# Five o tiles transposed by TensorE, seven loads moved on the SP queue, one projection moved ahead of the steps, in the first attention of a four-layer kernel

## The chip, the cores and the metric

The kernel runs on one core of a Trainium2 chip. The metric is the device time of one launch in microseconds. The time before is 1161.44 us, the median of three runs (1160.57, 1161.44, 1164.82). One further execution was profiled; all rows quoted below come from it.

Names of the engines: PE is TensorE (PEld are its weight loads), DVE is VectorE, ACT is ScalarE, POOL is GpSimd, SP is SyncE. SP, ACT and POOL also issue DMAs; "SPq" marks work on SP's queue.

## What is computed

Two kinds of layer in the order A, B, A, B, each with a layernorm in front and a residual around it, on x of 2048 rows and 576 columns in bf16. A is an attention of 32 heads of 18 columns in which each position sees itself and seven earlier positions at a distance of two. B is a gated MLP with a spatial projection.

```python
def _A_ref(x, wqkv, wo):
    B, S, D = x.shape
    H = 32
    Dh = D // H
    W, dil = (8, 2)
    qkv = (lambda x, *d: x.transpose(*d))((x @ wqkv).reshape(B, S, 3, H, Dh), 2, 0, 3, 1, 4)
    q, k, v = (qkv[0], qkv[1], qkv[2])
    ...
    logits = jnp.einsum('bhsd,bhswd->bhsw', q, kg) * scale
    logits = jnp.where(mask[None, None, :, :], logits, -1000000000.0)
    attn = _softmax(logits, axis=-1)
    o = jnp.einsum('bhsw,bhswd->bhsd', attn, vg)
    return (lambda x, *d: x.transpose(*d))(o, 0, 2, 1, 3).reshape(B, S, D) @ wo

x = A_x
x = x + _A_ref(_layernorm(x, axis=-1), A_wqkv, A_wo)
x = x + _B_ref(_layernorm(x, axis=-1), B_w_in, B_w_sp, B_b_sp, B_w_out)
x = x + _A_ref(_layernorm(x, axis=-1), A_wqkv, A_wo)
x = x + _B_ref(_layernorm(x, axis=-1), B_w_in, B_w_sp, B_b_sp, B_w_out)
```

## The kernel before

The attention layer (`layer_A`, called with `li` 0 and 2) sets the order of every engine by hand: within it each engine executes its instructions in the order in which the Python code emits them, and waits where an operand isn't there. The first call, `li == 0`, is the one that the change touches. It has three parts.

*The prologue.* x comes in by rows (`x_load`), is normalised on DVE (`S_`, `R_`, `A_`) and turned into `xnT`, tiles 0 to 3 by TensorE (`T_pe`), tiles 4 to 15 by DMA transposes on SP (`T_`, L306). `PG` (L482) projects q and k: one unit is a block `d` of 128 of the 576 columns, `qk` (0 or 1, q or k), and a chunk `cc` of 512 positions; it is five matmuls on TensorE (L462) and a copy into a staging buffer (L443 on DVE, L445 on ACT). Blocks 0 to 2 are staged in `stg`, block 3 of the second half in a buffer called `x_in` in the rows, block 4 and the first half's block 3 in a part of `win2a` that is lent out until its weights are loaded. When the last unit of a block is staged, its heads are moved by eight or so DMAs into `QK`, where each head has 18 of 32 partitions; these are issued alternately by POOL and SP (rows `QK<-stg`, `QK<-x_in`, `QK<-win2a`). The other 14 partitions hold a pattern that masks the window; DVE writes it in two halves (`fill_window_rows`, L201), after a load of the pattern (`win_pat`). `VW` projects v (L451).

A DMA's issue on POOL or SP waits until the DMA issued eight places before it by that queue kind has landed: there are eight completion semaphores on each.

*The steps.* The sequence is cut into 17 query tiles, one of 128 and sixteen of 120 positions; a step `s` (0 to 33) is half the heads of tile `s // 2`. Each step emits the logits of the next step (`L_mm`, 16 matmuls, L536) and their `EXP` on ACT (L545), then its own `PV` (16 matmuls, L559), after which DVE takes the reciprocal of the sums (L565) and writes o into one of four buffers `o_t` (L567); and then what a table holds for that step. The logits lie in PSUM in tag X (three banks, one buffer) and Y (one bank, two buffers). All else that TensorE writes (`O_ps`, `pp`, `pv`, `pw`, `pt`) takes turns on three banks, PT, during the steps. In the table stand:

- `PG`, the projections of the second half of the positions, one per step in steps 0 to 11, after six such units (`pre`) ahead of step 0; the order is (4,0,2), (3,1,2), (3,0,2) and then blocks 0, 1, 2, 3, 4 of the last chunk. The logits need the second half from step 16 on: step 16 takes blocks 0 to 2, step 17 blocks 2 to 4.
- `VW`, the rest of v, from step 12 on.
- `WO`, the output projection (L627, rows `pw`), from step 13 on, two halves per row tile, and behind it on DVE the residual sum (L630) and layernorm statistics (L638), on POOL the normalisation (L299), on SP the stores (`XST`, `XN_ST`); near the end SP reads the normalised rows back through DMA transposes (`LN_T`, L669) as `xnT` of the next layer, whose first matmuls are the rows `hh` (L234).
- `O_CP`: see next.

o has to be transposed for `WO`, into a ring `oT` of 768 columns. After the second half step of tile `t`, SP issues a DMA transpose of `o_t`: where the tile's first position is a multiple of 16 (tiles 0, 1, 3, 5, ...) right into the ring (L574, all 128 columns, of which the last eight belong to the next tile), otherwise into one of two slots (L578), from which DVE copies it some steps later (`O_CP`, L587). Only the last two tiles are transposed by TensorE (`O_T`, L593: five 128-column pieces into one PSUM bank, then a copy on ACT, L595).

*Loads.* At step 0 the table issues on SP the first three `XO` loads (rows of x for the residual, into `xo` and a part of `x_in`), and then `load_wo`. Two of the six pieces of `win2a`, weights of layer B that lie outside the part lent out, are loaded in the prologue from POOL's queue, between `R_(6, 2)` and the normalisation of tiles 6 and 7.

*After the steps* the tail of `WO` runs, and TensorE goes on with layer B.

Of the kernel before, what the change touches and what calls it, by code (L numbers as in the profile page):

```python
# [63 lines left out]
class K:  # L64
# [316 lines left out]
    def layer_A(self, li):  # L381
        nc, tc, cfg = self.nc, self.tc, self.cfg
        S, NT, XW, NS = cfg.S, cfg.NT, cfg.XW, cfg.NS
# [20 lines left out]
        oT = main.tile([P, 5, RING * P], bf16, name="oT")  # L404
# [17 lines left out]
        def tdim(t):  # L422
            return P, cfg.tiles[t][1]

        def q0_(t):
            return cfg.tiles[t][0]
# [14 lines left out]
        def evac(out, in_, dve):  # L441
            if dve:
                nc.vector.tensor_copy(out=out, in_=in_)  # L443
            else:
                nc.scalar.copy(out=out, in_=in_)  # L445
# [102 lines left out]
        def in_ring(t):  # L548
            return q0_(t) % 16 == 0

        def PV(s):
            t, hf = divmod(s, 2)
            nk, nq = tdim(t)
            O_ps = self.PT_tile([P, 512], f32, "O_ps")
            for jp, js in enumerate(((0, 1, 2), (3,))):
                for ftl in range(4):
                    for jj, j in enumerate(js):
                        idx = 4 * ftl + j
                        nc.tensor.matmul(O_ps[:, idx * (DH + 1):(idx + 1) * (DH + 1)],  # L559
                                         lhsT=P_bufs[2 * jp + s % 2][:nk, jj, ftl, :],  # L560
                                         rhs=v_ext[:nk, t, 16 * hf + idx, :], start=True, stop=True)
            Ov = O_ps[:, 0:16 * (DH + 1)].rearrange("p (h e) -> p h e", e=DH + 1)
            o_t = o_bufs[t % len(o_bufs)]
            rec = sb.tile([P, 16], f32, name="rec", tag="rec", bufs=2)
            nc.vector.reciprocal(out=rec[:], in_=Ov[:, :, DH])  # L565
            LN_AGGR()
            nc.vector.tensor_tensor(out=o_t[:, 288 * hf:288 * (hf + 1)].rearrange("p (h d) -> p h d", d=DH),  # L567
                                    in0=Ov[:, :, 0:DH], in1=rec[:, :, None].to_broadcast([P, 16, DH]), op=ALU.mult)
            LN_POW()
            if hf == 1 and t < NT - 2:  # L570
                if in_ring(t):
                    c0 = q0_(t) % (RING * P)
                    n0 = min(P, RING * P - c0)
                    nc.sync.dma_start_transpose(out=oT[:, :, c0:c0 + n0], in_=o_t[0:n0, :])  # L574
                    if n0 < P:
                        nc.sync.dma_start_transpose(out=oT[:, :, 0:P - n0], in_=o_t[n0:P, :])
                else:
                    nc.sync.dma_start_transpose(out=o_slots[(t // 2) % NSLOT][:], in_=o_t[:, :])  # L578

        def ring_parts(t):  # L580
            nq, c0 = tdim(t)[1], q0_(t) % (RING * P)
            n0 = min(nq, RING * P - c0)
            return [(c0, 0, n0)] + ([(0, n0, nq - n0)] if n0 < nq else [])

        def O_CP(t):
            for c0, a, n in ring_parts(t):
                nc.vector.tensor_copy(out=oT[:, :, c0:c0 + n], in_=o_slots[(t // 2) % NSLOT][:, :, a:a + n])  # L587

        def O_T(t):
            nq = tdim(t)[1]  # L590
            pt = self.PT_tile([P, 5, P], bf16, "pt")
            for c in range(5):
                nc.tensor.transpose(pt[:, c, :nq], o_bufs[t % len(o_bufs)][:nq, c * P:(c + 1) * P], self.ident[:nq, :nq])  # L593
            for c0, a, n in ring_parts(t):
                nc.scalar.copy(out=oT[:, :, c0:c0 + n], in_=pt[:, :, a:a + n])  # L595

        tails = {}
        late_rows = []
# [5 lines left out]
        def xo_of(p):  # L604
            if li == 0:
                return p % 3
            return p % 2 if p < 4 else (2, 0, 1)[(p - 4) % 3]

        def XO(i):
            if i % 2 == 0:  # L610
                xo = xo_bufs[xo_of(i // 2)]
                src = self.rows_of(x_prev, i, 2) if li == 0 else x_prev[i * P:(i + 2) * P, :]
                self.dma(xo, src.rearrange("(a p) d -> p a d", p=P), eng=nc.sync)
                for k_ in range(2):
                    tails[i + k_] = dict(xo=xo[:, k_, :])
# [25 lines left out]
        def LN_AGGR():  # L641
            for i, st in owed:
                mv = sb.tile([P, 2], f32, name="ln_mv", tag="ln_mv", bufs=5)
                nc.vector.bn_aggr(out=mv[:], in_=st[:])
                tails[i]["ln"] = mv

        def LN_POW():
            for i, _ in owed:
                mv = tails[i]["ln"]
                rstd = sb.tile([P, 1], f32, name="ln_rstd", tag="ln_rstd", bufs=5)  # L650
                nc.vector.tensor_scalar(out=rstd[:], in0=mv[:, 1:2], scalar1=EPS, scalar2=None, op0=ALU.add)
                nc.gpsimd.tensor_tensor(out=rstd[:], in0=rstd[:], in1=self.neg_half[:], op=ALU.pow)
                tails[i]["ln"] = mv, rstd, None
            owed.clear()
# [19 lines left out]
        if li == 0:  # L674
# [54 lines left out]
            def A_(*tiles):  # L729
                for i in tiles:  # L730
                    xns[i] = xn = self.xn_bufs[self.xn_rr % len(self.xn_bufs)]
                    self.xn_rr += 1
                    nc.vector.tensor_scalar(out=xn[:, 0:D], in0=xts[i], scalar1=mvs[:, i, 0:1],
                                            scalar2=rstds[:, i:i + 1], op0=ALU.subtract, op1=ALU.mult)
# [36 lines left out]
            S_(6, 7)  # L771
            R_(6, 2)
            rows[3](nc.gpsimd)
            for f in self.load_win2a(nc.gpsimd)[4:6]:
                f()
            A_(6, 7)
            T_(6, 7)
            S_(8)
# [49 lines left out]
        def at(s, f, *a):  # L828
            table.setdefault(s, []).append((f, a))
        pgs = [(d, qk, cc) for d, cc in ((0, 2), (1, 2), (2, 2), (0, 3), (1, 3), (2, 3), (3, 2), (3, 3), (4, 2), (4, 3))  # L830
               for qk in ((1, 0) if d < 4 else (0,))]
        PG_END = 14
        pre, pgs = pgs[:6], pgs[6:]
        if li == 0:
            pgs = [u for u in pgs if u[2] == 2] + [u for u in pgs if u[2] > 2]
            pgs.insert(0, pgs.pop(2))
        for k_, (d, qk, cc) in enumerate(pgs):
            at(k_ if li == 0 else (k_ * PG_END) // len(pgs), PG, d, qk, cc, True, *((q2,) if li == 0 else ()))
        vws = [(t, hh) for t in range(nvw, NT) for hh in range(2)]
# [7 lines left out]
        units += [NST] * 3 + [NST + 1] * 2 + [NST + 2] * 2  # L847
        wo_steps = list(zip(units[0::2], units[1::2]))
        assert len(wo_steps) == NS
        for t in range(NT - 2):  # L850
            s = wo_steps[q0_(t) // P][0] - 1
            r = (q0_(t) + tdim(t)[1] - 1) // P - RING
            if t < NT - 3 and not in_ring(t):
                at(min(2 * t + 6, s), O_CP, t)
                assert r < 0 or wo_steps[r][1] < min(2 * t + 6, s)
            else:
                assert r < 0 or wo_steps[r][1] < 2 * t + 1
        tail_rows = []
        for i in range(NS):
            s, s1 = wo_steps[i]  # L860
            if i % 2 == 0:
                last = [j for j in range(i) if xo_of(j // 2) == xo_of(i // 2)][-1:]
                at(max([s - 7 if li > 0 or last else 0] + [wo_steps[j][1] + 1 for j in last]), XO, i)
            at(s, WO, i, 0)
            at(s1, WO, i, 1)
            if s1 < NST - 1:
                at(s1, LN_STATS, i)
                at(s1 + 1, LN_XN, i)
            else:
                tail_rows.append(i)  # L870
            at(s1 + 1, XST, i)
            if i < NS - 2:
                at(s1 + 4, XN_ST, i)
            if NS // 2 <= i < NS - 1:
                for k_ in range(2):
                    at(max(s1 + 6, NST + 3 * (i - NS // 2) - 4, NST + 4 if i > NS // 2 + 1 else 0), LN_T, 2 * i - NS + k_)
# [7 lines left out]
            at(NST + 3, XN_ST, i)  # L884
        at(2 * (NT - 3) + 4, O_CP, NT - 3)
        if li == 0:
            at(0, self.load_wo, nc.sync)
            for k_ in range(4):
                at(PG_END - 1 + k_ if k_ else 1, self.load_win2a((nc.gpsimd, nc.sync)[k_ % 2])[k_])
        s_b, d_b = (PG_END + 3, 2) if li == 0 else (PG_END + 1, 1)  # L890
        at(s_b, alloc_win2b)
        for k_ in range(6):
            at(s_b + d_b * k_, win2b_piece, k_)
        at(NST - 2, O_T, NT - 2)
        at(NST, O_T, NT - 1)
        for k_, (d, qk, cc) in enumerate(pre):
            if k_ == (2 if li == 0 else 0):
# [9 lines left out]
        for s in range(NST):  # L907
            if s == NST - 1:
                self.ring = ["PT", "PT", "PT", "Y", "Y"]
            if s + 1 < NST:  # L910
                L_mm(s + 1)
                EXP(s + 1)
            PV(s)
            for f, a in table.pop(s, []):
                f(*a)
# [339 lines left out]
```

## Time and profile before

| | us |
|---|---|
| median of three runs | 1161.44 |
| the profiled execution, its time | 1159.11 |
| its span, first to last instruction | 1157.3 |
| TensorE busy | 1144.1 |
| first attention, to the first `hh` matmul of layer B | 127.0 |
| begin of step 0's `PV` | 49.6 |

The page gives, for one execution, the busy time of each engine, the chain of work that ended last, followed back from the last instruction, and groups of instructions by line. A timeline row is start, length, engine, line, operation, output and inputs, count, and in brackets the idle time of the engine in front of it with what ended it. A row of the chain in order of time is start, length and what the time went to; "issue" there is time in which an engine waited for nothing that the profile shows. A row of windows gives for a stretch the busy time of PE, PEld, DVE, ACT and POOL with the number of their instructions, then the granted TensorE clock (1.00 is full speed), the mean busy share of the DMA engines (it can exceed 1 where queues overlap), and GB/s. A row of waits is who waited for whom: us in total, times, longest. Line numbers are those of the kernel before.

### The profile page before, as it was taken

What the parts mean: (1) busy time and instruction counts of PE and PEld (TensorE: products, weight loads), DVE (VectorE), ACT (ScalarE), POOL (GpSimd) and SP (SyncE); (2) the same over time, 40 slices, a digit from 0 to 9 for tenths busy, and PEclk for the clock granted to TensorE, in tenths of its full rate; (3) what the DMA queues carried; (4) which work ended last, traced back from release to release, by engine and by line L of the source; (5) the groups of instructions that cost most, each with busy time, mean ns of one, the idle gap of its engine ahead of it and who ended that gap; (6) DMA issues with size and microseconds to landing.
All of it is one profiled execution on the core that took longest, in us unless ns stands there. A gap on an engine that the chain in (4) does not pass through costs nothing.

```text
span 1157.3 us, 29603 instructions
## 1 busy us (share of the span) xinstructions
PE 1144.1 (99%) x12894; PEld 613.0 (53%) x12894; DVE 535.3 (46%) x1184; ACT 371.3 (32%) x665; POOL 260.3 (22%) x389
## 2 busy tenths in 40 slices
PE   8989999999999999999999999999999999999998
PEld 5557644444444444457755774544444444444676
DVE  8768898222232222334475889853322223222311
ACT  5588656111110111102247886641111111011000
POOL 3669855000000000001254676530000000000000
PEclk9999999999999999999999999999999999999999
DMA  8798797000000000049455786940000000000322
GB/s 212 141 179 216 163 208 153 24 12 12 13 2 12 12 12 1 1 131 228 109 104 104 173 174 155 213 108 1 12 12 13 13 11 3 12 1 29 101 74 58
DMA packets 184637, 93.07 MB, mean 80 GB/s; under 512 B 136180, under 2 KB 177812, under 8 KB 184506
## 3 DMA queue, kind: packets, MB, share of 16 engines
q1 hardware_dynamic: 171866, 71.96, 29.6%
q0 software_dynamic: 6048, 13.31, 4.6%
q10 hardware_dynamic: 6592, 5.90, 1.7%
q8 instruction: 101, 1.65, 0.6%
q14 instruction: 30, 0.25, 0.1%
HBM read 35.46 MB, written 14.69 MB: 43 GB/s over the span
## 4 chain that ended last, share of the span: by engine, by line
PE 93%; DMA 3%; POOL 1%; DVE 1%; issue 1%; ACT 1%; SPq 0%; DVEq 0%; ACTq 0%; POOLq 0%
PE hh L234 79%; PE pp L462 4%; PE pw L627 3%; PE O_ps L559 2%; PE pv L451 2%; PE L_ps L536 2%; DMA QK<-stg 1%; POOL QK L78 1%; DMA QK<-x_in 1%; DMA x_in<-in_A_x_dram 1%; PE L_ps L462 1%; ACT P_sb L545 1%; DMA xnT<-ln_xn 0%; PE hh L1177 0%; DVE ln_st L713 0%
## 5 line engine op out<-in xcount | busy, mean ns | idle before, releaser
L234 PE MATMUL hh<-Wq,Z 64*128 64x512 bf16 x4608 | 505.8, 376 | 0.0
L234 PEld LDWEIGHTS <-Z 64*128 64x128 bf16 x6984 | 340.1, 94 | 309.8
L1081 DVE TENSOR_TENSOR g_tmp<-hh,ln_xn 128x512 f32<-128x512 f32 x144 | 92.8, 686 | 452.4 <-PE hh L234 452.4
L933 ACT COPY bank_turn<-ones 1x1 bf16<-1x1 bf16 x239 | 44.7, 187 | 538.3 <-PE hh L234 538.3
L78 POOL DMA_DIRECT2D wout<-in_B_w_out_dram x4 | 4.3, 1073 | 602.0 <-PE hh L234 602.0
L234 PE MATMUL hh<-wout,Z 64*128 64x288 bf16 x2232 | 137.0, 283 | 0.0
L545 ACT ACTIVATE P_sb<-L_ps 128x1440 bf16<-128x1440 f32 (+3 forms) x136 | 125.1, 972 | 23.5 <-PE L_ps L536 22.0
L234 PE MATMUL hh<-xnT,w 64*128 64x512 bf16 x1152 | 132.2, 376 | 0.0
L234 PE MATMUL hh<-win2a,xnT 64*128 64x512 bf16 (+1 forms) x960 | 118.7, 355 | 0.0
L234 PEld LDWEIGHTS <-xnT 64*128 64x128 bf16 x1440 | 69.9, 94 | 70.0 <-issue 0.5
L1006 DVE BATCH_NORM_STATS2 z_st<-zp 128x6 f32<-128x512 bf16 (+1 forms) x160 | 92.6, 622 | 11.1 <-ACT zp L1004 11.1
L1072 ACT ACTIVATE z1T<-hh 128x1024 bf16<-128x1024 f32 x72 | 73.7, 1023 | 62.2 <-PE hh L234 62.2
L1082 DVE TENSOR_TENSOR Z<-g_tmp,z1T 128x512 bf16<-128x512 f32 x144 | 92.3, 682 | 0.0
L234 PEld LDWEIGHTS <-w 64*128 64x128 bf16 x1152 | 56.1, 94 | 68.3
L1004 ACT ACTIVATE zp<-hh 128x1024 bf16<-128x1024 f32 (+1 forms) x96 | 76.0, 809 | 48.9 <-PE hh L234 48.7
L462 PE MATMUL pp<-xnT,wqk_sb 128*128 128x512 bf16 (+1 forms) x330 | 75.9, 379 | 1.7 <-DMA xnT<-ln_xn 1.7
L234 PE MATMUL hh<-win2b,xnT 64*128 64x512 bf16 (+1 forms) x480 | 72.8, 355 | 0.0
L1146 DVE TENSOR_TENSOR x_new<-hh,xo 128x288 bf16<-128x288 f32 x64 | 26.3, 452 | 92.7 <-PE hh L234 85.0
L299 POOL TENSOR_SCALAR ln_xn<-x_new,ln_mv,ln_rstd 128x576 bf16<-128x576 bf16 x28 | 64.1, 2288 | 2.6
L78 POOL DMA_DIRECT2D QK<-stg x76 | 48.0, 634 | 41.4 <-DVE stg L443 16.3
L462 PEld LDWEIGHTS <-wqk_sb 128*128 128x128 bf16 (+1 forms) x360 | 31.9, 97 | 38.5 <-issue 4.1
L1030 POOL TENSOR_SCALAR Z<-zp,z_mv,z_rstd 128x256 bf16<-128x256 bf16 x32 | 51.1, 1597 | 3.5
(122 smaller groups left out, 745.9 us busy)
## 6 DMA issues: line engine op xcount, KB each, us to landing
xres<-x_new SPq DMA_DIRECT2D x44, 144.0 KB
wout<-in_B_w_out_dram POOLq DMA_DIRECT2D x4, 1296.0 KB, 7.9
xo<-xres SPq DMA_DIRECT2D x32, 144.0 KB
xn_rows<-ln_xn SPq DMA_DIRECT2D x28, 160.0 KB
w<-in_B_w_in_dram SPq DMA_DIRECT2D x16, 256.0 KB
QK<-stg POOLq DMA_DIRECT2D x51, 72.0 KB, 4.6
QK<-stg SPq DMA_DIRECT2D x37, 72.0 KB
xo<-in_A_x_dram SPq DMA_DIRECT2D x6, 288.0 KB
```

Source lines behind the costliest of these rows:

```text
L78: return eng.dma_start(out=out, in_=in_)
L234: ins = self.nc.tensor.matmul(outs[a_], lhsT=lhs(a_, c, r0), rhs=rhs(a_, c, r0), start=start and k_ == 0, stop=stop and k_ == len(chunks) ...
L299: e.tensor_scalar(out=xn[:nrows, 0:D], in0=x_t[:nrows, :], scalar1=mv[:nrows, 0:1], scalar2=rstd[:nrows, 0:1], op0=ALU.subtract, op1=ALU.mult)
L462: nc.tensor.matmul(pp, lhsT=w, rhs=self.xnT[r0:r1, c, cc * 512:(cc + 1) * 512], start=start, stop=stop, tile_position=(r0, 0))
L545: nc.scalar.activation(out=P_bufs[2 * jp + s % 2][:nk, :, :, 0:nq], in_=Lv[:nk, :, :, 0:nq], func=ACT.Exp, scale=scale)
L933: self.turn_on = lambda tok: nc.scalar.copy(out=tok, in_=self.ones[0:1, 0:1])
L1004: nc.scalar.activation(out=zp[:, w0:w0 + n], in_=pz, func=ACT.Gelu_apprx_tanh)
L1006: nc.vector.bn_stats(out=st[:, x // 512, :], in_=zp[:, x:x + min(512, w0 + n - x)])
L1030: eng.tensor_scalar(out=Z[:, b0:b1, i, :], in0=zv[:, b0:b1, :], scalar1=mv[:, 0:1], scalar2=rstd[:, 0:1], op0=ALU.subtract, op1=ALU.mult)
L1072: lambda ht, z1T=z1T, q2=q2: nc.scalar.activation(out=z1T[:, q2 * 512:(q2 + 2) * 512], in_=ht[:].rearrange("p a b -> p (a b)"), func=ACT.G ...
L1081: nc.vector.tensor_tensor(out=tmp[:], in0=pg[:, a_, :], in1=bsp[:, qs], op=ALU.add)
L1082: nc.vector.tensor_tensor(out=uT(jj)[:, sub, qs], in0=tmp[:], in1=z1Ts[jj, sub][:, qs], op=ALU.mult)
```

## The change

All of it holds for the first attention alone (`li == 0`). Tiles 2 to 6 get no DMA transpose and no `O_CP`; instead `O_T` runs for tile t at the end of step 2t + 2, its copy on DVE (two copies for tile 6, which wraps around the ring's end). One unit, (3,1,2), moves from step 1 of the table to the end of `pre`, so that the units left stand in steps 0 to 10, each one step earlier; being the seventh there, its copy is made by ACT. The first three `XO`, `load_wo` and the two pieces of `win2a` are issued on SP where the table is built, that is behind the row transposes of tiles 12 to 15 and ahead of `pre`; the two pieces of `win2a` leave POOL's queue.

```diff
-            if hf == 1 and t < NT - 2:
+            if hf == 1 and t < NT - 2 and t not in pe_turn:
                 if in_ring(t):
...
+        pe_turn = tuple(range(2, 7)) if li == 0 else ()
+
         def O_T(t):
             nq = tdim(t)[1]
             pt = self.PT_tile([P, 5, P], bf16, "pt")
             for c in range(5):
                 nc.tensor.transpose(pt[:, c, :nq], o_bufs[t % len(o_bufs)][:nq, c * P:(c + 1) * P], self.ident[:nq, :nq])
             for c0, a, n in ring_parts(t):
-                nc.scalar.copy(out=oT[:, :, c0:c0 + n], in_=pt[:, :, a:a + n])
+                evac(oT[:, :, c0:c0 + n], pt[:, :, a:a + n], t in pe_turn)
...
             rows[3](nc.gpsimd)
-            for f in self.load_win2a(nc.gpsimd)[4:6]:
-                f()
             A_(6, 7)
...
         pre, pgs = pgs[:6], pgs[6:]
         if li == 0:
+            pre.append((3, 1, 2))
+            pgs.remove((3, 1, 2))
+        if li == 0:
             pgs = [u for u in pgs if u[2] == 2] + [u for u in pgs if u[2] > 2]
-            pgs.insert(0, pgs.pop(2))
+            pgs.insert(0, pgs.pop(1))
...
+        for t in pe_turn:
+            at(2 * t + 2, O_T, t)
         for t in range(NT - 2):
             s = wo_steps[q0_(t) // P][0] - 1
             r = (q0_(t) + tdim(t)[1] - 1) // P - RING
-            if t < NT - 3 and not in_ring(t):
+            if t in pe_turn:
+                assert s >= 2 * t + 2 and (r < 0 or wo_steps[r][1] < 2 * t + 2)
+            elif t < NT - 3 and not in_ring(t):
                 at(min(2 * t + 6, s), O_CP, t)
...
                 last = [j for j in range(i) if xo_of(j // 2) == xo_of(i // 2)][-1:]
-                at(max([s - 7 if li > 0 or last else 0] + [wo_steps[j][1] + 1 for j in last]), XO, i)
+                if li > 0 or last:
+                    at(max([s - 7] + [wo_steps[j][1] + 1 for j in last]), XO, i)
+                else:
+                    XO(i)
...
         if li == 0:
-            at(0, self.load_wo, nc.sync)
+            self.load_wo(nc.sync)
+            for f in self.load_win2a(nc.sync)[4:6]:
+                f()
```

## The prediction

> **What bounds the kernel now.** I read the page's busy times first, then the windows of the first attention (0 to 127 us), then the chain of work in order of time there, and last the timelines of TensorE, DVE, GpSimd and SP around each wait.
>
> ```profile
> span 1157.3 us, 29603 instructions
> ...
> PE 1144.1 (99%) x12894; PEld 613.0 (53%) x12894; DVE 535.3 (46%) x1184; ACT 371.3 (32%) x665; POOL 260.3 (22%) x389
> ```
>
> TensorE is busy for 1144.1 of 1157.3 us. So an edit in the first attention can only remove TensorE's waits there, or its slow stretches, or add TensorE work. Behind the first attention TensorE's program is the same before and after, so I let a gain made there reach the end whole.
>
> The chain in order of time (start, length, what) shows the largest wait:
>
> ```profile
> 68.85 7.71 DMA QK<-stg
> ...
> 77.41 7.70 DMA QK<-x_in
> ...
> 85.16 0.23 PE L_ps L536 x4
> ...
> 86.51 1.17 PE pw L627 x5
> 87.68 0.52 PE L_ps L536 x16
> 88.20 0.53 PE O_ps L559 x16
> 88.73 1.21 PE pv L451 x5
> ...
> 90.56 0.32 PE L_ps L536 x16
> 90.89 0.50 PE O_ps L559 x16
> 91.38 0.63 PE pv L451 x5
> 92.01 0.61 PE pw L627 x5
> ```
>
> The logits of step 17 need the heads of projection block d=3 (staged in x_in), whose moves into QK land at 85.11. TensorE's own timeline (start, length, what, idle before and its releaser):
>
> ```profile
> 47.95 0.46 PE L536 MATMUL L_ps<-QK 32*128 32x128 bf16 x13
> 48.84 0.84 PE L536 MATMUL L_ps<-QK 32*128 32x128 bf16 x3 [0.44 <-DMA QK<-win2a]
> ...
> 74.74 0.39 PE L536 MATMUL L_ps<-QK 32*128 32x120 bf16 x16 [0.40 <-ACT P_sb L545]
> ...
> 81.50 0.39 PE L536 MATMUL L_ps<-QK 32*128 32x120 bf16 x7
> ```
>
> Those logits begin at 81.50 and end at 85.16 + 0.23 = 85.39; an undisturbed step takes 0.32 for them: 3.57 us lost. The rows behind are slow: 1.17 against 0.61, 0.52 against 0.32, 0.53 against 0.50, 1.21 against 0.63, together 1.37 us; the granted clock of that window, 0.57, shows why. The hole costs 4.94 us. In these windows the busy times are followed by the granted clock, the DMA share and GB/s:
>
> ```profile
> 50.00:54.00 4.00, 4.00 (x83) 2.21 (x80) 3.66 (x7) 3.54 (x5) 1.32 (x3) 1.00 0.10 23
> 58.00:62.00 4.00, 4.00 (x77) 2.12 (x76) 2.95 (x8) 3.84 (x5) 1.98 (x4) 1.00 1.26 312
> 62.00:72.00 10.00, 9.57 (x186) 5.19 (x185) 7.18 (x16) 9.59 (x11) 6.49 (x12) 1.00 1.15 151
> 86.00:90.00 4.00, 4.00 (x49) 2.56 (x47) 2.90 (x10) 3.02 (x4) 3.38 (x5) 0.57 0.71 213
> ```
>
> DMA stands nearly idle from 50 to 54, and is full (a share over 1) while the moves that TensorE waits for are on their way.
>
> **The change, part by part.**
>
> *Start of the steps.* Two loads of win2a (288 KB each) leave GpSimd's queue, where they are issued while SP issues the last row transposes of tiles 4 to 7. Rows of DVE's and TensorE's timelines, and one of the chain:
>
> ```profile
> 24.99 0.43 DVE L733 TENSOR_SCALAR ln_xn<-oT,lnx_mv,lnx_rstd 128x576 bf16<-128x576 bf16 x1 [0.58 <-DMA xnT<-ln_xn]
> 25.10 9.87 PE L462 MATMUL pp<-xnT,wqk_sb 128*128 128x512 bf16 x45 [1.74 <-DMA xnT<-ln_xn]
> 25.97 2.36 DVE L201 COPY QK<-win_pat 128x4096 bf16<-128x4096 bf16 x2 [0.55 <-DMA win_pat<-win_period]
> 28.46 2.35 DVE L201 COPY QK<-win_pat 128x4096 bf16<-128x4096 bf16 x2
> 29.29 1.63 POOL QK L78
> ```
>
> TensorE waits 1.74 us for those transposes; DVE's normalisation and the fill of the window rows (L201) wait 0.58 and 0.55 behind the same traffic. Without these 0.59 MB TensorE can gain 0 to 1.74. But the steps start with the logits of step 1, and these waited for moves out of win2a (row 48.84), the end of a row of GpSimd issues. The first of that row, at 29.29, took 1.63 us and ended at 30.92, just behind the fill, 28.46 + 2.35 = 30.81. So the moves shift with the fill, and the fill with its two waits: 0 to 0.58 + 0.55 = 1.13 us. The loads removed are a large part of the traffic waited for, so I take 0.9. [...]
>
> *One projection out of the steps.* Five matmuls, 9.87/9 = 1.10 us, move in front of the logits of step 1. TensorE could have ended those at 47.95 + 0.33 = 48.28 and ended them at 48.84 + 0.84 = 49.68: 1.40 us of cover, so cost 0. Its copy goes to ACT, ahead of the second EXP. If the cover were gone (the moves earlier by more than TensorE), it would cost up to 1.10; both shifts have one cause, so I take 0. What it buys: every later projection comes one step earlier, 0.32 + 0.50 + 1.10 = 1.92 us. The step that loses its projection doesn't get shorter by it, since EXP sets a step's least length: the step before 74.74, which has no projection, still waited 0.40 for EXP.
>
> *Loads behind the row transposes, and the o tiles on TensorE.* The rows for both, from the timelines of SP and DVE, from the chain, and from the groups by form (busy us, mean ns, idle):
>
> ```profile
> 44.19 5.19 SPq L306 DMA_TRANSPOSE xnT<-ln_xn  x4
> 59.04 0.69 DVE L443 CAST stg<-pp 128x512 bf16<-128x512 f32 x1 [0.41 <-PE pp L462]
> 71.06 0.34 DVE L587 COPY oT<-o_slot 128x600 bf16<-128x600 bf16 x1
> 124.39 0.27 PE pt L593 x5
> L593 PE MATMUL pt<-ident,o_t 120*128 120x120 bf16 x10 | 0.9, 216 | 0.0
> ```
>
> SP issues the last row transposes until 44.19 + 5.19 = 49.38. Seven loads now stand right behind: three of xo (288 KB each), wo (576 and 72) and two of win2a (288 each), 2.09 MB, or 6.7 us at the 312 GB/s of the window 58 to 62. They begin where the DMA share is 0.10. On SP they pass two moves of block d=4, which only the logits of step 17 need, some 25 us later; behind them queue the o transposes of tiles 0 and 1 and the moves of d=0, first due at about 57. The loads are through by about 56: cost 0. One thing hangs on that: DVE's copy of tile 2 must wait for tile 1's transpose, as both write columns 248 to 255 of oT. That transpose, due at about 57, has until about 62 to land; later than that, DVE would stand and TensorE behind it, one us for each.
>
> Of the o tiles' 25 transposes, five take 0.27 between two groups of pw (row 124.39). They come in steps 6, 8, 10, 12 and 14. Step 12 covers its 0.27 with the 0.40 wait for EXP; the others are dense: +4 x 0.27 = 1.08 (all uncovered: 1.35). DVE copies them out, 600 elements each from PSUM, for which there is no row: between 0.34 (SBUF to SBUF, 600) and 0.69 x 600/512 = 0.81 (f32 from PSUM). I take 0.8, the row from PSUM being the nearer. DVE idles 0.41 in a projection step; two steps give 0.82, the longer step 0.27 more, and only every second step has a copy: cost 0. Were it not covered, 0.4 a tile, 2.0 us. DVE is rid of four slot copies.
>
> *The hole at 81.5.* TensorE now reaches the logits of step 17 at 81.50 - 0.9 + 1.08 = 81.7. The moves of d=3 start 1.92 + 0.9 earlier, less two transposed tiles ahead of them (0.54): at unchanged transfer times they land at 85.1 - 2.3 = 82.8. The remaining 1.1 us must come from DMA. At the 151 GB/s of the window 62 to 72 it moves 3.0 MB in the 20 us from 62 to 82; five transposes of 160 KB are 0.8 MB of it, 27%, and the loads in front are gone by then. Two transfers of 7.7 us stand one behind the other in that chain: 27% off each would be 4.2 us, so I take the hole as gone, -4.94. At unchanged transfers it is -3.8, and -2.5 if the clock falls all the same: these are the bounds.
>
> *Waits without a cause.* TensorE's waits list two in the same full windows that nothing in the profile explains:
>
> ```profile
> PE O_ps L559 <- issue: 0.4, 1, 0.4
> PE L_ps L536 <- issue: 0.3, 1, 0.3
> ```
>
> Between 0 and -0.7; they occur only where DMA is full, so I take -0.7.
>
> Sum: -4.94 - 0.7 + 1.08 - 0.9 = -5.46 us. The profiled execution took 1159.11 (its span of 1157.3 and 1.8 around it): 1153.65. The median of the runs shown, 1161.44, is 2.33 above that execution, so the median comes to 1156.0, 0.47% less. About 0.5%, 5.8 us, is what a measurement of this kernel can tell from no change: the forecast stands just inside.
>
> **Rivals.**
>
> *The transfers get no quicker.* The moves are small pieces, and 7.7 us may be their own time. Then 1.1 us of the wait is left and the waits without a cause stay: 1156.0 + 1.1 + 0.7 = 1157.8, or 1159.2 if the clock falls too. For it: two of 7.7 in series, one like the other. Against it: the share over 1, a sign that they queue.
>
> *Nothing gained at the start.* If the row transposes take their time in any case, 0.9 falls out: 1156.9, with the waits without a cause 1157.6. For it: SP needs 5.19/4 = 1.3 us just to issue one. Against: 0.59 MB ran beside them.
>
> *Slower: the transposes cost more than their row.* Place: steps 6 to 14. If each of the 25 ran alone at its mean of 216 ns instead of overlapped, they would take 5.4 instead of 1.08, +4.3; if each group also drew the clock down as the hole did, 5 x 1.37 = 6.9 more: -5.46 + 11.2 = +5.7, 1167.2. It decides from the point where a group takes over 0.27 + 5.46/5 = 1.36 us. Against it: five in 0.27 at 124.39. [...]
>
> **How the numbers follow.** Forecast 0.58; transfers no quicker 0.15; nothing at the start 0.20; slower 0.07. The best sum, -4.94 - 0.7 + 1.08 - 1.13, ends at 1155.8; single runs of the three shown lie 0.9 below and 3.4 above their median, and SP, rid of five issues of 1.3 us, may give something that I did not count, so the range starts at 1153.0. Upward it takes in the first two rivals: 1160.0. Faster by over 0.5% means under 1155.6: not quite half of the forecast's cases, and of the second rival's those with a gain not counted: 0.42. Within 0.5%: 0.51. Slower by over 0.5%: 0.07.
>
> **What would show it.** Right: no wait of L_ps for QK near 80 us and no window there under a clock of 1.00; five groups of pt at about 0.27; the wait at 25.10 shorter, and the first O_ps of the steps before 49; DMA busy from 50 on, its share between 62 and 82 lower. Wrong: DMA xnT or a DVE copy into oT as releaser of TensorE in the steps; or a wait of the first hh rows of the next layer for xnT, which would hand the gain back.

## The result, and the profile after

The changed kernel takes 1154.95 us in the median (1154.50 to 1158.79), the kernel before 1161.38 beside it: a ratio of 0.9956, 95% interval [0.9935, 0.9976]. The forecast was 1156.0 with 1153.0 to 1160.0 as its range.

The execution that was profiled took 1158.59 us, one of the two longest of seven. Against the profiled execution of before (1159.11) it gained 0.52 us only. The page shows the same bound as before:

```profile
span 1156.8 us, 29646 instructions
...
PE 1143.2 (99%) x12919; PEld 613.5 (53%) x12919; DVE 536.4 (46%) x1185; ACT 372.2 (32%) x666; POOL 259.9 (22%) x387
```

The same windows as were shown of before:

```profile
50.00:54.00 4.00, 3.74 (x78) 2.00 (x67) 2.97 (x7) 3.35 (x5) 3.03 (x7) 1.00 0.86 237
58.00:62.00 4.00, 4.00 (x87) 2.33 (x79) 2.99 (x7) 3.84 (x5) 3.10 (x6) 1.00 1.45 173
62.00:72.00 10.00, 8.07 (x155) 4.77 (x152) 6.01 (x14) 6.96 (x9) 5.14 (x10) 1.00 0.89 140
86.00:90.00 4.00, 4.00 (x86) 2.96 (x84) 3.32 (x12) 3.77 (x6) 3.05 (x5) 1.00 1.08 213
```

DMA works from 50 on (0.86 instead of 0.10), is less full between 62 and 72 (0.89 instead of 1.15), and the slow stretch at 86 is gone (clock 1.00 instead of 0.57). But TensorE is busy for 8.07 of the ten microseconds from 62 to 72, where it was 9.57. TensorE's waits over the whole execution and rows of its timeline name what came (line numbers from here on are those of the kernel that the row belongs to):

```profile
PE O_ps L559 <- issue: 2.4, 2, 1.3
PE O_ps L559 <- DVE oT L443: 1.8, 1, 1.8
PE L_ps L536 <- ACT P_sb L545: 1.5, 3, 1.0
```

```profile
48.24 0.56 PE L559 MATMUL O_ps<-v_ext,P_sb 128*128 128x19 bf16 x16
...
82.93 0.39 PE L536 MATMUL L_ps<-QK 32*128 32x120 bf16 x16
...
105.49 0.35 PE L559 MATMUL O_ps<-v_ext,P_sb 128*128 128x19 bf16 x8 [1.31 <-issue]
...
113.06 0.30 PE L559 MATMUL O_ps<-v_ext,P_sb 128*128 128x19 bf16 x6 [1.07 <-issue]
...
126.67 0.82 PE L234 MATMUL hh<-win2a,xnT 64*128 64x512 bf16 x6
```

The first `O_ps` comes at 48.24 (49.62 before). The logits of step 17, row 82.93, run through in one piece: no wait for QK, the hole is gone. In its place stand a wait of 1.82 us for DVE's copy into oT and two stalls that the profile puts down to nothing. The chain of work in order of time, and DVE's timeline:

```profile
27.88 1.64 POOL QK L78
...
57.09 8.37 DMA oT<-o_t
...
65.54 0.47 DVE oT L443
...
67.98 0.27 PE pt L595 x5
```

```profile
27.05 2.35 DVE L201 COPY QK<-win_pat 128x4096 bf16<-128x4096 bf16 x2
...
65.54 0.47 DVE L443 COPY oT<-pt 128x600 bf16<-128x600 bf16 x1 [3.04 <-DMA oT<-o_t]
```

This is the hazard that the prediction named, and its own sign of being wrong, a DVE copy into oT that releases TensorE: tile 1's DMA transpose, in flight for 8.37 us behind the 2.09 MB, lands at 65.46 instead of by 62. DVE stands 3.04 us in front of its copy of tile 2, and the reciprocal and the `o_t` queued behind that copy keep TensorE from its next `O_ps`.

Step by step it reads as follows. A step is the time from its first logits matmul (those of the step after it) to the next step's, out of TensorE's timeline; "again" is a second profiled execution of the changed kernel, first below.

| us | before | after | again |
|---|---|---|---|
| start of step 1 | 51.21 | 49.83 | 49.97 |
| step 2 | 1.92 | 2.25 | 2.25 |
| steps 6 and 10, each | 1.92 | 2.18 | 2.18 |
| step 8 | 1.92 | 4.36 | 2.76 |
| step 11 | 2.49 | 1.92 | 1.91 |
| step 14 | 2.06 | 2.71 | 2.72 |
| step 15 | 2.64 | 2.06 | 2.06 |
| steps 16 and 17 together | 9.00 | 4.11 | 4.11 |
| steps 26, 28 and 29 together | 6.16 | 8.96 | 6.17 |
| start of step 32 to the first `hh` | 7.75 | 8.03 | 8.03 |
| first `hh` | 127.03 | 126.67 | 122.41 |
| the execution's time | 1159.11 | 1158.59 | 1154.19 |

The execution's time less its first `hh` is nearly the same in all three (1032.08, 1031.92 and 1031.78), so the first `hh` tells what an execution gained.

### The profile page after: what moved, and what is told of

It reads as the page before. It is cut to its first block, busy times and chain, and to the rows that moved or that the text cites. A ratio compares the mean times of both kernels' runs of the same rounds, so it can differ in the third digit from the quotient of the medians.

```text
span 1156.8 us, 29646 instructions
## 1 busy us (share of the span) xinstructions
PE 1143.2 (99%) x12919; PEld 613.5 (53%) x12919; DVE 536.4 (46%) x1185; ACT 372.2 (32%) x666; POOL 259.9 (22%) x387
## 3 DMA queue, kind: packets, MB, share of 16 engines
q0 software_dynamic: 5888, 12.72, 4.7%
q8 instruction: 101, 1.65, 0.6%
## 4 chain that ended last, share of the span: by engine, by line
PE 94%; POOL 1%; DMA 1%; ACT 1%; DVE 1%; issue 1%; DVEq 0%; ACTq 0%; POOLq 0%
PE hh L234 79%; PE pp L462 4%; PE pw L629 3%; PE pv L451 3%; PE O_ps L559 2%; PE L_ps L536 2%; POOL QK L78 1%; ACT P_sb L545 1%; DMA oT<-o_t 1%; PE L_ps L462 1%; DMA QK<-win2a 0%; PE hh L1189 0%; DVE ln_st L640 0%; ACT xnT L744 0%; DVE x_new L632 0%
```

## The experiments

Twelve measurements, in three series of four; the kernels of a series ran on one chip beside the kernel before, which had a median of 1160.68, 1158.70 and 1159.04 in them. Ratios are to that, with 95% intervals.

**The changed kernel once more.** No edit.

> The changed kernel once more. Theory A (the change as forecast: the hole in front of the logits of step 17 goes, the steps start 1 to 1.4 us earlier, and the late landing of tile 1's o transpose seen in the first profile, which held DVE for 3.0 us and TensorE for 1.8, is the accident of a disturbed execution): median 1154 to 1156, and if the profiled execution is one of the quick ones (under 1156) its trace has no wait of TensorE for the oT copy above 0.3 us, and its first hh matmul starts before 123. Rival B (the late landing is there in every execution and the quick ones differ elsewhere): a quick execution's trace has the wait of 1.5 to 2 us all the same, first hh at 124 or later.

Median 1155.18 (1153.80 to 1159.13), ratio 0.9954 [0.9938, 0.9970]. The profiled execution, 1154.19, is 4.40 us shorter than the first. Its waits in the steps, and two pieces of its chain:

```profile
PE L_ps L536 <- ACT P_sb L545: 1.3, 2, 1.0
PE O_ps L559 <- ACT P_sb L545: 0.4, 1, 0.4
PE L_ps L536 <- DMA QK<-win2a: 0.3, 1, 0.3
PE O_ps L559 <- DVE oT L443: 0.3, 1, 0.3
```

```profile
56.53 7.46 DMA oT<-o_t
...
64.09 0.47 DVE oT L443
```

The transpose lands 1.5 us earlier, at 63.99, and the wait is 0.3, as theory A has it; no stall by "issue" is left. The 4.26 us between the two executions of one program, at the first `hh`, are step 8 (1.60) and steps 26, 28 and 29 (2.79), less 0.14 at the start.

**The loads alone.** The seven loads of the change on the kernel before, no tile turned, no projection moved:

```diff
-            for f in self.load_win2a(nc.gpsimd)[4:6]:
-                f()
...
-                at(max([s - 7 if li > 0 or last else 0] + [wo_steps[j][1] + 1 for j in last]), XO, i)
+                if li > 0 or last:
+                    at(max([s - 7] + [wo_steps[j][1] + 1 for j in last]), XO, i)
+                else:
+                    XO(i)
...
-            at(0, self.load_wo, nc.sync)
+            self.load_wo(nc.sync)
+            for f in self.load_win2a(nc.sync)[4:6]:
+                f()
```

> The kernel before with the moved loads alone (the two of win2a off GpSimd's queue, xo, wo and win2a behind the row transposes on SP). Theory A: the steps start 1.0 to 1.4 us earlier; the moves of d=3 and TensorE both shift by that, so the wait for the QK moves at step 17 stays at 2 to 3.6 us with its slow clock: median 1.0 to 2.5 below the kernel before. Rival C (the hole comes from the loads that stood in front of the moves, DMA relief at 50 to 60 us is what closes it): no wait of L_ps for QK moves left, 5 to 6.5 us below.

Median 1158.10 (1155.85 to 1161.58), ratio 0.9975 [0.9959, 0.9990]. The steps start at 48.64, and the hole stays; TensorE's timeline:

```profile
82.17 0.23 PE L536 MATMUL L_ps<-QK 32*128 32x120 bf16 x2 [0.80 <-DMA QK<-x_in]
82.90 0.22 PE L536 MATMUL L_ps<-QK 32*128 32x120 bf16 x1 [0.50 <-DMA QK<-x_in]
83.43 0.23 PE L536 MATMUL L_ps<-QK 32*128 32x120 bf16 x2 [0.31 <-DMA QK<-x_in]
84.28 0.23 PE L536 MATMUL L_ps<-QK 32*128 32x120 bf16 x4 [0.62 <-DMA QK<-x_in]
```

So the loads go with an earlier start and do not remove the hole: steps 16 and 17 take 8.82 together, where before they took 9.00.

**The turned tiles alone.** `pe_turn`, the `O_T` in the table and the copy on DVE; loads and projection as before.

> The kernel before with the five o tiles on TensorE alone. Theory A: +1.1 us of TensorE; the moves start no earlier (0.5 later for the two tiles ahead), their transfers get up to 27 per cent shorter, so the hole shrinks to 0 to 2 us without slow clock: 1.5 to 4.5 us below the kernel before. Rival D (transfers keep their 7.7 us whatever shares DMA with them): the hole stays at 2.5 to 3.5 us with slow clock, and the time is the kernel before's plus 0 to 1 us.

Median 1156.88 (1154.44 to 1161.79), ratio 0.9972 [0.9958, 0.9986]. There is no wait for QK at step 17, though GpSimd issues its moves of block d=3 later than before (77.5 to 79.8 instead of 73.8 to 77.4). Their row in the DMA view of 48 to 86 us (KB each, median us from issue to landing), of the kernel before and then of this one:

```profile
QK<-x_in POOLq DMA_DIRECT2D x4, 72.0 KB, 7.9
```

```profile
QK<-x_in POOLq DMA_DIRECT2D x4, 72.0 KB, 3.1
```

With five DMA transposes fewer the same moves land in less than half the time. But TensorE came late to step 17 in this execution (its logits begin at 87.36 instead of 81.50), which by itself makes a wait less likely; the last of the experiments compares without this. The profiled execution is a long one (1160.12). Its chain, TensorE's timeline and two windows:

```profile
58.80 9.24 DMA oT<-o_t
```

```profile
68.65 0.58 PE L559 MATMUL O_ps<-v_ext,P_sb 128*128 128x19 bf16 x16 [3.70 <-DVE oT L443]
```

```profile
66.00:70.00 4.00, 1.18 (x17) 0.76 (x18) 1.84 (x5) 0.88 (x2) 1.16 (x2) 0.61 0.87 133
70.00:74.00 4.00, 3.86 (x43) 2.05 (x43) 2.26 (x6) 1.25 (x1) 1.00 (x2) 0.53 0.35 78
```

With wo and xo right in front of the o transposes on SP, tile 1's lands at 68.04; the wait is 3.70, and the clock falls to 0.53 behind it. Steps 8 and 9 take 9.97 instead of 4.09: 5.88 us for a wait of 3.70.

**The projection alone.** On the kernel before:

```diff
+            pre.append((3, 1, 2))
+            pgs.remove((3, 1, 2))
...
-            pgs.insert(0, pgs.pop(2))
+            pgs.insert(0, pgs.pop(1))
```

> The kernel before with one projection moved ahead of the steps alone. Theory A: the moves start 1.92 us earlier at unchanged transfers: the wait at step 17 shrinks from 3.6 to 1.7 us, and the slow clock behind it goes: 1.9 to 3.3 us below the kernel before; start of the steps unchanged within 0.2. Rival D: the same, since it only needs unchanged transfers. Rival E (one step earlier is enough, because GpSimd no longer issues behind its own waits): the wait gone whole, 4.5 to 5 us below.

Median 1159.60 (1157.28 to 1162.36), ratio 0.9988 [0.9977, 1.0000]: hardly told apart from no change. Rival E's gain of 4.5 us lies outside the interval; theory A's 1.9 lies inside, near its end. The wait for block d=3 is 1.8 us in five pieces where it was 2.6 in four. But in this execution TensorE came to it late, as step 11 shows (timeline, then a window):

```profile
73.77 0.32 PE L559 MATMUL O_ps<-v_ext,P_sb 128*128 128x19 bf16 x6 [3.18 <-issue]
```

```profile
74.00:78.00 4.00, 4.00 (x77) 2.62 (x74) 2.42 (x7) 2.86 (x3) 2.16 (x4) 0.50 1.26 134
```

So this trace can't say how much of the shorter wait is the projection's.

**Turned tiles and projection, without the loads.** The changed kernel with the seven loads put back to where they were.

> The changed kernel with the seven loads put back to where they were (two of win2a on GpSimd's queue, wo and xo in the first steps); the turned tiles and the moved projection stay. Theory A (the hole goes by five fewer DMA transposes and the earlier block d=3, the start by the loads): the steps start at about 49.6 again, 1.4 us later than with the loads moved; no wait of L_ps for QK<-x_in over 0.3 us near 80 us, granted clock 1.00 there; total about 1.4 us above the changed kernel, 1155.9 to 1157. Rival B (the loads' early start is what frees DMA for the moves of d=3): a wait of L_ps for QK<-x_in of 1 us or more comes back, clock under 1.00 near 82 us, total 1158 or more. Rival C (the loads do nothing): start at 48.3, total as the changed kernel within 0.5.

Median 1160.57 (1157.65 to 1165.08), ratio 1.0022 [1.0007, 1.0037]: slower than before. Only theory B has a total as high as that, and its reason is not there: no wait for QK<-x_in came back. The first `O_ps` is at 49.13, and the time went into one wait that none of the three theories has (TensorE's waits; then two windows):

```profile
PE O_ps L559 <- DVE oT L443: 3.4, 1, 3.4
```

```profile
66.00:70.00 4.00, 1.21 (x18) 0.78 (x19) 1.98 (x6) 1.04 (x2) 1.15 (x2) 0.85 0.84 125
70.00:74.00 4.00, 4.00 (x49) 2.06 (x52) 2.11 (x5) 1.47 (x2) 3.38 (x6) 0.72 0.80 154
```

Step 8 takes 7.17 instead of 2.18. If that wait is what made it slow, what the loads' new place buys above all is that they are out of the way of tile 1's transpose. The next experiment followed from this: turn tiles 0 and 1 on TensorE too, and no DMA transpose writes oT in these steps.

**Tiles 0 to 6 on TensorE.** The changed kernel with

```diff
-        pe_turn = tuple(range(2, 7)) if li == 0 else ()
+        pe_turn = tuple(range(0, 7)) if li == 0 else ()
```

> The changed kernel with the tiles 0 and 1 turned by TensorE too, so that no DMA transpose writes oT before tile 7. Theory A (the late landing of tile 1's DMA transpose holds DVE's copy of tile 2, and by that TensorE, by 1.8 us in the profiled execution of the changed kernel and 0.3 in a quicker one): the wait of O_ps for DVE's copy into oT is under 0.3 us in any execution; TensorE does 2 x 0.27 = 0.54 us more; first hh matmul at 122.4 to 123.2 if nothing else stands; median 0 to 1.5 us under the changed kernel. Rival (DVE is simply late there, whatever transpose is in flight): a wait of 1 us or more for the copies into oT stays, median 0.5 us above the changed kernel.

Median 1154.85 (1154.05 to 1156.34), ratio 0.9970 [0.9957, 0.9983]. No wait for a copy into oT is in the trace, and step 8 takes 2.17. The changed kernel itself was not in this series, so both were run once more, below.

**Every transpose twice.** The changed kernel with

```diff
-            for c in range(5):
+            for c in list(range(5)) * (2 if t in pe_turn else 1):
```

> The changed kernel with each of the 25 transposes of the tiles 2 to 6 done twice, into the same place. Theory A (a group of five costs TensorE 0.27, pipelined): each group takes about 0.5 to 0.55 instead of 0.27, total +1.1 to +1.4 us, about 1156.4, the clock stays at 1.00 in the steps. Rival (each costs its 216 ns alone): +5.4 us, about 1160.4; with the clock drawn down too, 1165 or more.

Median 1155.70 (1154.48 to 1159.06), ratio 0.9982 [0.9970, 0.9994]. Two groups of ten and what follows each, in TensorE's timeline:

```profile
62.14 0.69 PE L595 MATMUL pt<-ident,o_t 120*128 120x120 bf16 x10
62.77 0.39 PE L536 MATMUL L_ps<-QK 32*128 32x120 bf16 x16
...
66.78 0.69 PE L595 MATMUL pt<-ident,o_t 120*128 120x120 bf16 x10
67.40 0.39 PE L536 MATMUL L_ps<-QK 32*128 32x120 bf16 x16
```

From the start of ten to the next logits it is 0.63 and 0.62, where five of the changed kernel take 0.36 (67.82 to 68.18): five more cost 0.27. The rival's 1160.4 or more is out. One window differs: from 74 to 78 the clock was 0.60, behind a stall of 0.56 and a wait of 1.03 for EXP; the changed kernel had the same wait for EXP without a drop. Whether the doubled transposes had a part in it, one trace can't say.

**Only win2a back on GpSimd's queue.** The changed kernel with the two loads of win2a in the prologue; xo and wo stay behind the row transposes.

> The changed kernel with only the two loads of win2a put back on GpSimd's queue in the prologue; xo and wo still begin behind the last row transposes. Theory A (these two loads ran beside the last row transposes and held back DVE's normalisation and window fill, hence GpSimd's moves and the start of the steps): DVE's fill starts at about 26.0 instead of 24.6, a TensorE wait of about 1.7 us for xnT at 25 us is back, first O_ps at about 49.6 instead of 48.3, total about 1.4 us above the changed kernel. Rival (the start came from elsewhere, as from the projection moved in front or from an accident of the execution): first O_ps stays at 48.3 to 48.5, total within 0.4 of the changed kernel.

Median 1155.65 (1154.13 to 1160.38), ratio 0.9972 [0.9954, 0.9990]. The start moved as theory A has it and further; the ratio can't be told apart from the changed kernel's. TensorE's timeline:

```profile
50.32 0.56 PE L559 MATMUL O_ps<-v_ext,P_sb 128*128 128x19 bf16 x16
```

The fill on DVE starts at 25.68, and the wait for xnT is back with 1.22. With less on SP in front of it, tile 1's transpose holds nobody up (step 8: 2.18). Over all fourteen traces the first `O_ps` stands at 49.35 in the mean of the six kernels with these loads in the prologue (48.45 to 50.32) and at 48.60 in the eight without (47.92 to 49.53): 0.75 us, with a scatter between traces as large. TensorE's wait for xnT near 25 us parts the two sorts more clearly: it is 0.82 to 1.74 in each of the six, and in the eight it is listed once, with 0.45.

**Four on one chip.** Tiles 0 to 6 with the loads as before the change; the changed kernel; tiles 0 to 6 again; and tiles 0 to 6 with the projection left in the steps.

> The tiles 0 to 6 turned by TensorE and the moved projection, but the seven loads where they were before the change. Theory A (what made the kernel without the moved loads slow is tile 1's DMA transpose, which landed 3.4 us late behind those loads; with that gone the loads are worth only the start, about 1 us): no wait for a copy into oT of over 0.3 us, first hh matmul at 123 to 124.5, median 0.5 to 1.5 us above the kernel with tiles 0 to 6 turned and the loads moved. Rival B (the late loads cost more than that, by other moves that land late): first hh at 126 or later, a new wait for a DMA in the steps, median 2.5 us or more above.

> The changed kernel as it is, beside the next two on one chip. Theory A: ratio to the kernel before 0.994 to 0.997, single runs spread over 4 us or more, since tile 1's transpose lands late in some executions.

> The changed kernel with tiles 0 and 1 turned by TensorE too, on the same chip as the changed kernel. Theory A: median 0 to 1.5 us under the changed kernel, single runs within about 2.5 us of one another, since no copy into oT waits for a DMA. Rival: as the changed kernel in median and in spread.

> Tiles 0 to 6 turned by TensorE and the loads moved, but the projection left in the steps. Theory A (the projection costs nothing in front and buys nothing once five or more DMA transposes are gone): no wait of L_ps for QK<-x_in, a wait of L_ps for QK<-win2a of 0.4 to 1.0 us at the first steps in the projection's place, the wait of 1.0 us for EXP near 74 us gone, median within 0.7 us of the kernel with the projection moved. Rival B (without its earlier start the block d=3 is late again): a wait for QK<-x_in of 1 us or more near 81 us, median 2 us or more above.

| | median | single runs | ratio | first `hh` in the trace |
|---|---|---|---|---|
| tiles 0 to 6, loads as before | 1155.63 | 1154.04 to 1159.60 | 0.9967 [0.9952, 0.9983] | 123.45 |
| the changed kernel | 1155.74 | 1153.50 to 1158.40 | 0.9968 [0.9950, 0.9986] | 124.94 |
| tiles 0 to 6 | 1155.09 | 1153.66 to 1156.64 | 0.9962 [0.9947, 0.9976] | 122.57 |
| tiles 0 to 6, no projection moved | 1154.87 | 1153.32 to 1157.48 | 0.9959 [0.9940, 0.9977] | 121.43 |

The first row answers for the fifth experiment, from which it differs by tiles 0 and 1 alone: with their DMA transposes gone, the loads in their old place no longer make the kernel slower than before. They cost 0.54 us against the third row, which lies within the intervals. TensorE has no wait for a copy into oT in its trace. Nor does DVE wait before its copy of tile 2 with the loads moved (timeline of the third row):

```profile
63.13 0.46 DVE L443 COPY oT<-pt 128x600 bf16<-128x600 bf16 x1
```

The gain of tiles 0 to 6 over the changed kernel is 0.65 in the median, within the intervals. It shows in the tail: of 26 runs of the changed kernel in all its series four were above 1158, of 24 runs of "tiles 0 to 6" none was above 1156.64. The single runs of its second series lie 2.98 apart, a little more than the expected 2.5.

The last row answers for the projection: theory A holds. No wait for QK<-x_in comes back. TensorE's waits in the steps, of "tiles 0 to 6" and then of the kernel without the move:

```profile
PE L_ps L536 <- ACT P_sb L545: 1.0, 1, 1.0
PE O_ps L559 <- ACT P_sb L545: 0.4, 1, 0.4
PE L_ps L536 <- DMA QK<-win2a: 0.4, 1, 0.4
PE pw L629 <- DVE ln_rstd L653: 0.2, 1, 0.2
```

```profile
PE L_ps L536 <- DMA QK<-win2a: 0.6, 1, 0.6
PE pw L629 <- DVE ln_rstd L653: 0.2, 1, 0.2
```

The move leaves a step without a projection, and 1.03 us of waiting for EXP in its place. In the median it makes no difference that can be measured (0.22).

This last kernel also closes the question of the hole. From "the loads alone" it differs only by its turned tiles, and TensorE comes to the logits of step 17 at the same time, 80.64 here and 80.82 there. The moves of block d=3, in the DMA view of 48 to 86 us, of the loads alone and then of this kernel:

```profile
QK<-x_in POOLq DMA_DIRECT2D x4, 72.0 KB, 8.4
```

```profile
QK<-x_in POOLq DMA_DIRECT2D x4, 72.0 KB, 3.3
```

There the logits wait 2.2 us for these moves, here not at all. The moves gain twice: GpSimd, whose issues wait for its earlier moves to land (4.9 us in six waits for QK<-stg in the kernel before), also gets to its last one of this block at 73.1 instead of 76.3.

## Why the prediction was right, point by point

The median came within 1.1 us of the forecast, and the second trace's execution within 0.6 of the sum made for one (1154.19 against 1153.65). The mechanism of the largest term was right. That the number came out as near is partly luck: in the second trace costs of about 1.6 us that the sum doesn't have stand against gains of about 0.7 that it has too small, and the gain in the median was 6.43 us in the first comparison, 5.50 and 3.30 in the two later ones. The terms, each as predicted and as the two traces of the changed kernel have it against the steps of before:

| us | predicted | after | again |
|---|---|---|---|
| start of step 1 | -0.9 | -1.38 | -1.24 |
| hole (steps 16, 17) | -4.94 | -4.89 | -4.89 |
| stalls without a cause (steps 11, 15, 26, 28, 29) | -0.7 | +1.65 | -1.15 |
| turned tiles (0.26 each in 6, 8 and 10; step 14) | +1.08 | +1.43 | +1.44 |
| wait for tile 1's transpose (rest of step 8) | 0 | +2.18 | +0.58 |
| projection (step 2, the tail) | 0 | +0.61 | +0.61 |
| sum | -5.46 | -0.40 | -4.65 |
| first `hh`, measured | | -0.36 | -4.62 |

*The hole.* Right in size and in cause: DMA transposes stood in the way of the moves. With the same loads, and TensorE at the same place at the same time, the moves take 8.4 us and are waited for when tiles 0 to 6 go by DMA, and take 3.3 and are not when TensorE turns these tiles. In the changed kernel, with five tiles turned, they take 5.2 and 5.5 in the two traces instead of 7.9: about a third less, where the prediction had 27%. "Transfers no quicker" falls by that.

*The turned tiles.* Right for a group: 0.26 by the steps (2.18 against 1.92) and 0.27 by the doubling, which rules out the slower rival. Mis-sized in step 14, which takes 0.65 more. Its second half of `pw` waits for DVE there (0.22 in the waits); that wait is in no trace without turned tiles and in all with them but the one with groups of ten, whose step 14 is as long (2.71). The 0.8 taken for DVE's copy was wrong, it takes 0.46 to 0.47; in steps 6, 8 and 10 it was covered either way. The granted clock is 1.00 in every window read from the two traces of the changed kernel, those with the groups in them too (62 to 82).

*The start.* Right in direction; the size in one trace is partly scatter. Between the traces without and with the two win2a loads in the prologue lie 0.75 in the mean. The cap of 1.13 was passed (1.38): it counted DVE's two waits and not that a whole prologue runs up to about 0.9 us earlier or later from one trace to the next. That GpSimd's moves hang on the fill held: the first issue ended at 27.88 + 1.64 = 29.52, the fill at 29.40, so it ended 0.12 behind the fill, as it did by 0.11 before; what ties the one to the other no run shows. The loads alone, win2a put back and the wait for xnT in all fourteen traces speak against "nothing gained at the start".

*"The loads are through by about 56: cost 0."* This step failed. SP's last row transposes left SP a little earlier than before (49.27), but SP needed until 53.8 to issue the seven loads. In the four stretches of 2 us from 50 to 58 the DMA queue of the kind "hardware_dynamic" moved 0.35, 0.57, 0.56 and 0.57 MB, 2.05 in all, and all others 0.17. SP's transfers are in it: when the two loads of win2a went from GpSimd to SP, the queue "software_dynamic" fell from 13.31 to 12.72 MB, by their 0.59. So the 2.09 MB weren't through before about 58, by estimate. The seven loads, the moves and the transposes of tiles 0 and 1 kept DMA at a share of 1.45 until 62, and tile 1's transpose landed at 65.46 and 63.99, past the 62 that the prediction had given it. The hazard was named, and its price, one for one, was a little low for short waits (1.82 cost 2.18, and 0.26 cost 0.58); where the loads are not early, 3.4 and 3.7 cost 5.0 and 5.9, with the clock down to 0.72 and 0.53 behind them.

*"One projection: cost 0."* Mis-sized: 0.61. Its copy on ACT delays EXP in step 2 (0.33), and the shift of the steps makes the last `O_ps` wait 0.42 for EXP (0.28 in the tail). It was not needed for the hole either.

*"Waits without a cause: -0.7."* Right in direction in the second trace, where it was worth more: the two stalls listed before with 0.43 and 0.28 had lengthened their steps by 0.58 each. Wrong in the first trace, which had two of 1.31 and 1.07. They did not go with the full windows of before; see the last section.

## What to carry to other kernels

A transfer that writes even a few columns of what the next copy writes can be a wait in the schedule (here eight columns, and 0.26 to 3.70 us of TensorE): move its whole class to the other engine, or count where it lands behind the loads put in front of it. Parts of a change are not worth the sum of what each is worth alone: two of these parts together lost 0.2%, and the third, worth no more than about 0.5 us once the shared wait was removed, turned them into a gain of 0.3 to 0.5%. One profile of a kernel whose runs spread by 5 us is one draw; compare step by step with a second one before a missing gain is put down to the change.

## What the runs showed of the hardware that had not been expected

*Stalls at fixed places.* TensorE's stalls by "issue" come at the same instructions in both traces of the changed kernel that have them: behind eight matmuls of `O_ps` in step 26 and ten in step 29 (1.31 and 1.07; in the third trace, "the changed kernel" of the last series, 0.51 and 0.38; in the second none). Between the two lie 128 of TensorE's matmuls, and as many lie before, between the stalls at 71.63 and 79.36. Shortly in front of each, the DMA view has one packet on a queue of the kind "instruction". The windows 103.00 to 103.20 and 110.40 to 110.60 of the profiled execution of the changed kernel (packets, MB, share of 16 engines):

```profile
q8 instruction: 1, 0.02, 32.9%
```

```profile
q8 instruction: 1, 0.02, 32.9%
```

The stalls end at 105.49 and 113.06, about 2.5 us behind them. The kernel before has such packets at 68.7 and 76.6, and its stalls end at 71.63 and 79.36, 2.9 and 2.8 us behind. From the packet to where TensorE stopped it is 2.5 us in both cases there, and the stalls are 0.43 and 0.28; in the changed kernel it is 1.2 and 1.5, and the stalls are 1.31 and 1.07. So in these four the later the packet, the longer the stall. As many matmuls ahead of the first of them in the changed kernel, at 97.81, TensorE ran on: there the packet stands at 92.1, 5.7 us in front. Whether TensorE waited for what these packets brought, and why they come late, is open, and no run took the DMA load away at that place alone, so this is argued and not shown.

*The clock behind a wait.* After a wait of 1.82 us (the changed kernel, step 8) it stayed at 1.00; after 3.18, 3.37 and 3.70 us it fell to 0.50, 0.72 and 0.53 in the next windows. The loads alone had 0.74 from 86 to 90 with no wait over 0.83 but 2.2 us of them within the logits of one step, and the kernel before had 0.57 there with no wait over 1.01 but 2.6 us of them in that step. So here the longest single wait did not decide alone.

*Left open.* Why turned tiles and projection without the loads lost in every run what the turned tiles alone lost only in some (least single run 1157.65 against 1154.44) is not settled: both traces show the same wait (3.4 and 3.7), and each is one execution.
